# Last batch's down projection: each product of quarters made by seven products of sixteenths, weights stationary

## The chip, the core and the metric

The kernel runs on one core of a Trainium2 chip. TensorE (PE) multiplies matrices: it holds a stationary operand (`lhsT`), streams a moving one (`rhs`) past it, and adds up into PSUM. VectorE (DVE), ScalarE (ACT) and GpSimd (POOL) work element by element; POOL here works on SBUF only. SyncE (SP) issues most DMA transfers; ACT and POOL can issue some. Each engine works through its own queue in order and waits on semaphores of the others. The metric is the device time of one execution in microseconds.

## The reference

Attention with a mask by clusters, over 4 batches, 8 heads, 768 tokens and head size 64, and then a feed-forward block on the 3072 x 512 result:

```python
mask = q_assign[:, :, :, None] == k_assign[:, :, None, :]
scores = np.where(mask, scale * q @ k.T, -1e9)      # q, k: (4, 8, 768, 64)
x = softmax(scores) @ v                             # then bridged to (3072, 512)
h = x @ w_in                                        # w_in: (512, 2048)
g = h - np.tanh(h)
out = g @ w_out                                     # w_out: (2048, 512)
```

The change touches only the last line, and only for the last of the four batches (768 of the 3072 tokens). Everything is float32.

## The kernel before, in words

The feed-forward block is made batch by batch. Batch 0's second half and batches 1 to 3 use a Strassen-like scheme of seven products instead of eight: the matrices are cut into quarters, sums of quarters are made, seven products of quarters are computed, and the results are put together from them. The numbers 1 to 7 in `PRODUCTS` (L783) name the products.

For batches 1 to 3, `strassen_items(b)` (L992) lists the work as items. Its first 56 items are the up projection (`up_items`, L901): 8 blocks of rows `i`, seven products each, every product four matmul calls of 128x64 weights against 384 tokens (L933). The weights come as a *stream*: ready-made sums, one tile per block, fetched two ahead by `fetch_factors` (L844) on SP's queue into three buffers. VectorE evicts each product from PSUM and adds (L928). `shrink` (L997) makes tanh on ACT (L1000) and subtracts on POOL (L1002), and `done` (L1004) has POOL make one sum and one difference of quarters (L1007, L1008). The result lies in `G`, 2 x 2 quarters of 8 x 128 rows and 384 tokens, and in `S1` (`left1`).

Then come 21 items of the down projection: 7 products by 3 chunks of 128 tokens, `down_product` (L1014). There `G` or `S1` is stationary (128x64 halves) and the stream of w_out's sums is moving, 256 columns (L1029). Each item writes one PSUM tile (three buffers, `ps_f`). VectorE, or ACT for product 1 (L1035), evicts it into `du` or into `c` (L1040), POOL updates two quarters of `G` in place (L1036 after product 1, L1052 after product 2), and `put` sends finished 128 x 256 pieces to `out` (L1048), for the last batch by SP. All sums that this scheme needs of w_out are made once, early, and lie in DRAM (`down_factors`).

For batches 1 and 2 these items are threaded between the steps of the next batch's attention. For batch 3 nothing is left beside them: from L1376 on, the list `tail` runs alone, up projection first, then down projection, with a few checks between. The order of the instructions on each engine is the order in which the program emits them (a manual schedule). An item emits its matmuls, then its evictions; waits come from the data and from the buffers.

At the end of the program every engine waits for its queue, reads a flag and branches (L1561, L1562) past a general version.

Of the kernel before, what the change touches and what calls it, by code (L numbers as in the profile page):

```python
# [30 lines left out]
F32 = mybir.dt.float32  # L31
# [4 lines left out]
ALU = mybir.AluOpType  # L36
# [3 lines left out]
P = 128  # L40
# [18 lines left out]
def kernel(  # L59
# [10 lines left out]
    nc = tc.nc  # L70
# [3 lines left out]
    B, H, S, D = q.shape  # L74
# [3 lines left out]
    NCH = S // P  # L78
# [100 lines left out]
    def fast():  # L179
# [602 lines left out]
        HM = DM // 2  # L782
        PRODUCTS = (1, 2, 6, 7, 4, 5, 3)  # L783
        SLOT = {which: i for i, which in enumerate(PRODUCTS)}
        up_factors = dram.tile([HF, P, CH, 7, P], F32, name="up_factors", bufs=1)
        down_factors = dram.tile([7, P, HF, HM], F32, name="down_factors", bufs=1)

# [56 lines left out]
        def fetch_factors(n: int):  # L844

            if n < (B - 1) * PER:
                i = n + HF if n < 0 else n % PER
                t = streams[n] = late_pools["stream"].tile([P, HF, HM], F32, name="stream")
                if i < HF:
                    t = streams[n] = t.rearrange("p a b -> p (a b)")[:, 0 : 7 * CH * P].rearrange(  # L850
                        "p (c k f) -> p c k f", k=7, c=CH
                    )
                nc.sync.dma_start(t, up_factors[i] if i < HF else down_factors[i - HF])

        late_pools, half_pools, diffs = {}, {}, {}
        mid = ExitStack()
# [41 lines left out]
            ):  # L898
                nc.vector.tensor_tensor(out=out, in0=u, in1=w, op=ALU.subtract)  # L899

        def up_items(b: int, base: int, quarter, shrink, done):  # L901


            held = {}
            width = TB if b else TB // 2

            def up_product(i: int, k_: int, between):
                which = PRODUCTS[k_]
                x = [columns(b, c) for c in range(CD)]
                d = diffs[b] if which in (4, 5, 6) else None  # L910
                if which in (4, 5, 6):
                    right = [d[:, {5: 0, 6: 1, 4: 2}[which], c] for c in range(CH)]
                else:
                    rows_, half = {1: (0, 0), 2: (CH, 0), 3: (CH, 1), 7: (0, 1)}[which]
                    right = [x[rows_ + c][:, half] for c in range(CH)]
                if k_ == 0:
                    if b:
                        held[i] = (
                            late_pools["s"].tile([P, width], F32, name="s"),
                            late_pools["u"].tile([P, 2, width], F32, name="u"),  # L920
                        )
                    else:
                        t = turnp0.tile([P, 2, TB], F32, name="t1")
                        held[i] = t[:, 0, 0:width], t[:, 1].rearrange("p (a n) -> p a n", a=2)
                s, u = held[i]

                def add(out, x, y):
                    nc.vector.tensor_tensor(out=out, in0=x, in1=y, op=ALU.add)  # L928

                ps = ps_f.tile([P, TB], F32, name="pu", tag="f")[:, 0:width]  # L930
                for c in range(CH):
                    for r in halves:
                        nc.tensor.matmul(  # L933
                            ps[r], lhsT=streams[base + i][:, c, k_, r], rhs=right[c],
                            start=(c == 0), stop=(c == CH - 1),
                        )
                if which == 1:
                    nc.scalar.copy(out=s, in_=ps)
                elif which == 2:
                    add(quarter(i, 0, 0), ps, s)  # L940
                    if i == HF - 1:
                        shrink(i, 0, slice(0, 1))
                elif which == 6:
                    fetch_factors(base + i + 2)
                    add(u[:, 0], ps, s)
                elif which == 7:
                    add(u[:, 1], ps, u[:, 0])
                elif which == 4:
                    add(quarter(i, 1, 0), ps, u[:, 1])
                elif which == 5:  # L950
                    add(u[:, 0], ps, u[:, 0])
                    add(quarter(i, 1, 1), ps, u[:, 1])
                    shrink(i, 1, slice(0, 2))
                else:
                    add(quarter(i, 0, 1), ps, u[:, 0])

                    shrink(i, 0, slice(1 if i == HF - 1 else 0, 2))
                between()
                if k_ == len(PRODUCTS) - 1:
                    done(i)  # L960
                    streams.pop(base + i)


            return [
                (1.3 * width / TB, 1, lambda between, i=i, k_=k_: up_product(i, k_, between))
                for i in range(HF) for k_ in range(len(PRODUCTS))
            ]
# [6 lines left out]
        def half_up_items(gs):  # L974
# [13 lines left out]
                nc.gpsimd.tensor_tensor(out=t, in0=t, in1=th, op=ALU.subtract)  # L988

            return start_without(up_items(0, -HF, quarter, shrink, lambda i: None))  # L990

        def strassen_items(b: int):  # L992
            base = (b - 1) * PER
# [20 lines left out]
            def down_product(k_: int, j: int, between):  # L1014
# [49 lines left out]
                between()  # L1064


            return up_items(b, base, lambda i, f, t: G[:, i, f, t], shrink, done) + [
                (3.4, 2, lambda between, k_=k_, j=j: down_product(k_, j, between))
                for k_ in range(len(PRODUCTS)) for j in range(HCH)
# [526 lines left out]
```

## Time and profile before

| | |
|---|---|
| median of 3 runs | 957.5 us (956.85 to 958.44) |
| the profiled execution | 958.52 us, span of its instructions 956.7 us |
| PE busy | 941.8 us (98%) |
| DVE / ACT / POOL busy | 571.2 / 292.6 / 512.1 us |
| granted TensorE clock | 1.000 |
| last batch's up projection begins | at 805.38 us of the span |
| its down projection begins | at 877.98 us |
| the last eviction begins | at 950.71 us |

In the profile, "L1029 PE MATMUL pd<-stream,G 128*64 128x256 f32 x1728 | 191.2, 379" reads: line 1029 of the kernel, engine, operation, output tile and inputs, shapes, how many records, then busy time in us and the mean duration of one in ns. A float32 matmul call leaves two matmul records, each with a weight load of its own (PEld). "[2.31 <-ACT th L1000]" says that the engine stood idle for 2.31 us before, and what ended it. In a row of windows the columns are: stretch, its length, then busy us and number of instructions of PE, PEld, DVE, ACT and POOL, the granted clock, the share of DMA and GB/s.

### The profile page before, as it was taken

Reading aid. Unit: us, or ns where it says so; the run is one execution under the profiler, and the core shown is the slowest. Engines: PE = TensorE matmul, PEld = TensorE weight load, DVE = VectorE, ACT = ScalarE, POOL = GpSimd, SP = SyncE. Lnnn points to the kernel's source line nnn. Section 1 sums busy time; section 2 is a strip of 40 time slices with the busy share of each in tenths; the row PEclk is TensorE's granted clock in tenths of the full one; section 3 lists DMA queues with packets and bytes.
Section 4 is the critical chain, followed back from the end, with each engine's and each line's share of the span. In section 5 each row is a group of like instructions: output and inputs, shape, how many; then the busy total and the mean of one; then the engine's idle time right before and its main releaser. Section 6 shows DMA issues by size and latency. Waiting matters only on the chain.

```text
span 956.7 us, 16942 instructions
## 1 busy us (share of the span) xinstructions
PE 941.8 (98%) x6584; PEld 458.6 (48%) x6584; DVE 571.2 (60%) x1098; ACT 292.6 (31%) x453; POOL 512.1 (54%) x364
## 2 busy tenths in 40 slices
PE   8999999999999999999999999999999999999997
PEld 5433443345653333444455554444455555445664
DVE  7657676976776677666845567766754346443011
ACT  5575554223332332323321212333331220222000
POOL 1026353456775464777684453867796353657500
PEclk9999999999999999999999999999999999999999
DMA  7766455992736645474574746457334223323321
GB/s 196 200 188 147 141 153 128 261 258 88 196 117 157 158 143 122 151 175 130 189 191 148 181 146 184 111 179 173 110 125 146 98 81 103 116 78 132 107 106 36
DMA packets 166764, 139.85 MB, mean 146 GB/s; under 512 B 116580, under 2 KB 145044, under 8 KB 163988
## 3 DMA queue, kind: packets, MB, share of 16 engines
q1 hardware_dynamic: 160292, 117.15, 44.4%
q0 software_dynamic: 6240, 21.50, 6.8%
q8 instruction: 54, 0.88, 0.4%
q14 instruction: 34, 0.28, 0.1%
q10 hardware_dynamic: 144, 0.03, 0.0%
HBM read 117.48 MB, written 21.17 MB: 145 GB/s over the span
## 4 chain that ended last, share of the span: by engine, by line
PE 92%; DVE 2%; DMA 1%; ACT 1%; issue 1%; SPq 0%; DVEq 0%; ACTq 0%
PE pu L933 26%; PE pd L1029 23%; PE sc L499 14%; PE av L556 13%; PE o L746 8%; PE h L730 4%; PE sim L376 1%; DMA stream<-up_factors 1%; PE den L571 1%; PE den L617 1%; DVE e L531 1%; PE den L590 1%; DVE diff L899 0%; PE pq L432 0%; DVE t L348 0%
## 5 line engine op out<-in xcount | busy, mean ns | idle before, releaser
L547 POOL TENSOR_TENSOR sum<-sum,e 128x768 f32<-128x768 f32 x112 | 207.4, 1852 | 94.4 <-DVE e L531 90.2
L531 DVE SCALAR_TENSOR_TENSOR e<-row,code,sc 128x384 f32<-128x384 bf16 x336 | 185.9, 608 | 67.3 <-ACT sc L521 59.7
L521 ACT ACTIVATE sc<-sc 128x768 f32<-128x768 f32 x168 | 125.9, 789 | 229.5 <-PE sc L499 211.8
L1029 PE MATMUL pd<-stream,G 128*64 128x256 f32 x1728 | 191.2, 379 | 0.0
L933 PE MATMUL pu<-xT,stream 128*64 128x384 f32 (+1 forms) x1024 | 159.0, 447 | 1.7 <-DMA stream<-up_factors 1.1
L1029 PEld LDWEIGHTS pd<-stream,G 128*64 128x64 f32 x1728 | 123.9, 137 | 66.9 <-issue 7.2
L499 PE MATMUL sc<-t,t 64*128 64x384 f32 x768 | 150.2, 509 | 0.4 <-ACT e L521 0.3
L556 PE MATMUL av<-e,vals 128*64 128x384 f32 x768 | 145.9, 499 | 1.3 <-DVE e L531 1.3
L1002 POOL TENSOR_TENSOR G<-G,th 128x768 f32<-128x768 f32 (+1 forms) x51 | 87.1, 1724 | 69.4 <-ACT th L1000 69.2
L933 PE MATMUL pu<-diff,stream 128*64 128x384 f32 (+1 forms) x768 | 121.1, 448 | 2.8 <-DVE G L928 1.8
L933 PEld LDWEIGHTS pu<-xT,stream 128*64 128x64 f32 x1024 | 73.1, 137 | 75.8 <-issue 61.4
L499 PEld LDWEIGHTS sc<-t,t 64*128 64x128 f32 x768 | 65.9, 186 | 73.8 <-issue 37.6
L556 PEld LDWEIGHTS av<-e,vals 128*64 128x64 f32 x768 | 46.9, 136 | 86.3 <-issue 82.0
L1000 ACT ACTIVATE th<-G 128x768 f32<-128x768 f32 (+1 forms) x51 | 40.9, 806 | 148.9 <-DVE G L928 144.2
L543 POOL TENSOR_TENSOR sum<-e 128x768 f32<-128x768 f32 x28 | 52.6, 1879 | 62.8 <-DVE e L531 42.2
L746 PE MATMUL o<-w_out,g 128*64 128x512 f32 x384 | 86.1, 593 | 0.0
L933 PEld LDWEIGHTS pu<-diff,stream 128*64 128x64 f32 x768 | 53.8, 137 | 59.3 <-issue 45.2
L928 DVE TENSOR_TENSOR G<-pu,u 128x384 f32<-128x384 f32 x72 | 39.7, 552 | 32.9 <-PE pu L933 32.9
L1040 DVE SCALAR_TENSOR_TENSOR c<-pd,du 128x256 f32<-128x256 f32 x36 | 15.2, 421 | 67.1 <-PE pd L1029 67.1
L746 PEld LDWEIGHTS o<-w_out,g 128*64 128x64 f32 x384 | 27.4, 137 | 50.1 <-issue 50.0
L1040 DVE SCALAR_TENSOR_TENSOR du<-pd,du 128x256 f32<-128x256 f32 x27 | 11.4, 420 | 60.8 <-PE pd L1029 60.8
L730 PE MATMUL h<-xT,w_in 128*64 128x384 f32 x256 | 42.8, 486 | 0.0
(137 smaller groups left out, 827.0 us busy)
## 6 DMA issues: line engine op xcount, KB each, us to landing
stream<-up_factors SPq DMA_DIRECT2D x32, 896.0 KB
stream<-down_factors SPq DMA_DIRECT2D x21, 1024.0 KB
raw<-in_moe_w_in_dram POOLq DMA_DIRECT2D x16, 512.0 KB, 5.0
raw<-in_moe_w_out_dram POOLq DMA_DIRECT2D x16, 512.0 KB, 4.7
again<-in_moe_w_in_dram SPq DMA_DIRECT2D x32, 256.0 KB
again<-in_moe_w_out_dram SPq DMA_DIRECT2D x32, 256.0 KB
vals<-in_v_dram SPq DMA_DIRECT2D x32, 192.0 KB
row<-q_codes SPq DMA_DIRECT2D x29, 192.0 KB
```

The source lines that it names most:

```text
L499: nc.tensor.matmul(sc[i][:, h, 0:TB], lhsT=turned[n, 1][r].rearrange("p a n -> p (a n)")[:, j * P : (j + 1) * P], rhs=turned[n, 0][r, half ...
L521: nc.scalar.activation(out=out, in_=sc[i][:, :, 0:TB], func=ACT.Exp, scale=SCALE)
L531: nc.vector.scalar_tensor_tensor(out=e[:, h].rearrange("p (j n) -> p j n", n=P), in0=rows[n, half][:, h], scalar=(codes[n][:, h, 1, j : j ...
L543: nc.gpsimd.tensor_tensor(out=s, in0=pair[0], in1=pair[1], op=ALU.add)
L547: nc.gpsimd.tensor_tensor(out=s, in0=s, in1=pair[i], op=ALU.add)
L556: nc.tensor.matmul(avs[n, half][h * D : h * D + D], lhsT=vals[n][:, h, j], rhs=e[i][:, h], start=(j == 0), stop=(j == NCH - 1),)
L730: nc.tensor.matmul(h[r], lhsT=w_in[i][:, c, o * P : (o + 1) * P][:, r], rhs=xT[c][:, half], start=(c == 0), stop=(c == CD - 1),)
L746: nc.tensor.matmul(acc[sub][r], lhsT=gs[f % HF][:, f // HF, sub * P : (sub + 1) * P][:, r], rhs=w_out[f // FQ][:, f % FQ], start=(f == seq ...
L933: nc.tensor.matmul(ps[r], lhsT=streams[base + i][:, c, k_, r], rhs=right[c], start=(c == 0), stop=(c == CH - 1),)
L1000: nc.scalar.activation(out=th, in_=t, func=ACT.Tanh)
L1002: nc.gpsimd.tensor_tensor(out=t, in0=t, in1=th, op=ALU.subtract)
L1029: nc.tensor.matmul(ps[r], lhsT=left(i)[:, r], rhs=t[:, i], start=(i == 0), stop=(i == HF - 1))
```

## The change

Only the last batch's down projection is made in another way (`wide_items`). Each of the seven products of quarters is itself computed by seven products of sixteenths, in the same scheme one level deeper: 49 parts instead of 21 items. A part multiplies 192 tokens by 4 x 128 rows by 128 columns. The operands change sides: a sixteenth of the w_out stream is stationary (128x64 halves), and the tokens are moving, so a part comes out with output columns on partitions and tokens along them. PSUM tiles rotate over six buffers of three pools.

The sums of sixteenths are not in DRAM; they are made on the fly. For the next product, POOL makes four right-hand sums (`right_sums`, 512 elements per partition each) from its stream, and VectorE makes four left-hand sums (`left_sums`, 768 elements each), the third of them on POOL in two of the seven products. All of these have both inputs in SBUF. POOL's updates of `G` after products 1 and 2 are cut in four pieces of 768 elements each. The first product's sums are made during the up projection on VectorE (`aside`). For that the blocks are visited in the order 0, 4, 1, 5, 2, 6, 3, 7, and the products come in the order 1, 7, 2, 6, 4, 5, 3.

The seven parts of a product are added by VectorE on their way out of PSUM, ACT taking the first. The products are joined by VectorE sums of 768 elements (`joins`). As the result lies turned, VectorE turns it back in blocks of 32 x 32 (`transpose`), and it is stored in transfers whose pieces are 32 floats, four per half of a quarter on SP. The last quarter goes in four pieces, shared by SP and ACT.

Within a product, the work that is not needed at once (joins, left-hand sums) is spread over the seven parts behind their evictions. The diff, cut to its core:

```diff
+        BLOCKS = tuple(i + k_ * HF // 2 for i in range(HF // 2) for k_ in range(2))
+        WIDE = (1, 7, 2, 6, 4, 5, 3)
+        PARTS = (1, 2, 6, 7, 5, 4, 3)
...
-                nc.sync.dma_start(t, up_factors[i] if i < HF else down_factors[i - HF])
+                if i < HF:
+                    nc.sync.dma_start(t, up_factors[BLOCKS[i] if last else i])
+                else:
+                    nc.sync.dma_start(t, down_factors[SLOT[WIDE[i - HF]] if last else i - HF])
...
+            def left_sums(k_: int, engine, i=None):
...
+                l11, l12, l21, l22 = (left(k_, t, f, i) for t in range(2) for f in range(2))
+                return [
+                    lambda e=e, out=out, x=x, y=y, op=op: e.tensor_tensor(out=out, in0=x, in1=y, op=op)
+                    for e, out, x, y, op in (
+                        (nc.vector, s[5], l21, l22, ALU.add),
+                        (nc.vector, s[6], s[5], l11, ALU.subtract),
+                        (engine, s[7], l11, l21, ALU.subtract),
+                        (nc.vector, s[3], l12, s[6], ALU.subtract),
+                    )
+                ]
...
+            def right_sums(k_: int, engine):
...
+                r11, r12, r21, r22 = (right(k_, f, n) for f in range(2) for n in range(2))
+                return [
+                    lambda out=out, x=x, y=y: engine.tensor_tensor(
+                        out=out, in0=x, in1=y, op=ALU.subtract
+                    )
+                    for out, x, y in (
+                        (t[5], r12, r11), (t[6], r22, t[5]), (t[7], r22, r12), (t[4], r21, t[6]),
+                    )
+                ]
+
+            def aside(at: int, k_: int):
+                if at % 2 == 0 and at and 2 <= k_ < 6:
+                    left_sums(0, nc.vector, at // 2 - 1)[k_ - 2]()
+                if at == HF - 1:
+                    if k_ == 2:
+                        aux["right"] = right_sums(0, nc.vector)
...
+            def updates(which: int):
+                x, y = {1: ((0, 0), None), 2: ((1, 0), (0, 0))}[which]
+                def chunk(i: int):
+                    ks = slice(2 * i, 2 * i + 2)
+                    a = G[:, ks, x[0], x[1]]
+                    if y is None:
+                        nc.gpsimd.tensor_tensor(out=a, in0=left1[:, ks], in1=a, op=ALU.subtract)
...
+            def store(t: int, m: int, n: int, x=None):
...
+                for a in range(P // BL):
+                    queue = nc.scalar if x is not None and a % 2 else nc.sync
+                    queue.dma_start(out_b[b, t, m, n, a, :, ks], q_[a * BL : (a + 1) * BL, n, ks])
...
+            def part(k_: int, slot: int):
+                kind, final = PARTS[slot], k_ == len(WIDE) - 1
+                if slot == 0:
+                    fetch_factors(base + HF + k_ + 2)
+                    ready_ = joins(k_ - 1) if k_ else []
...
+                    if not final:
+                        for it in right_sums(k_ + 1, nc.gpsimd):
+                            it()
+                        ready_ += left_sums(k_ + 1, nc.vector if changed else nc.gpsimd)
+                    if k_ and WIDE[k_ - 1] in changed:
+                        for it in updates(WIDE[k_ - 1]):
+                            it()
...
+                for i in range(KH):
+                    for r in range(2):
+                        nc.tensor.matmul(
+                            ps[r * D : r * D + D], lhsT=w[:, i, r * D : r * D + D], rhs=x[:, i],
+                            start=(i == 0), stop=(i == KH - 1),
+                        )
...
+                def add(out, y):
+                    nc.vector.scalar_tensor_tensor(
+                        out=out, in0=ps, scalar=float(words), in1=y, op0=ALU.mult, op1=ALU.add
+                    )
...
+                ready_ = aux["ready"]
+                share = -(-len(ready_) // (len(PARTS) - slot))
+                for it in ready_[:share]:
+                    it()
+                del ready_[:share]
...
+            if b == B - 1:
+                aside, items = wide_items(b, base, G, left1)
+                return up_items(
+                    b, base, lambda i, f, t: G[:, i, f, t], shrink, done, BLOCKS, aside
+                ) + items
```

## The prediction

> **What bounds the kernel now.** I read four views. First the page: its slices say TensorE is busy everywhere at the full granted clock, so the end moves only with TensorE's work or with a new wait on it.
>
> ```profile
> PE   8999999999999999999999999999999999999997
> PEclk9999999999999999999999999999999999999999
> ```
>
> Second, the chain that ended last, from 860 us on: one up projection, then 72.5 us of down products without a gap, one eviction, the end. The waits ahead of the last batch cannot move by this edit.
>
> ```profile
> 859.76 18.38 PE pu L933 x114
> 878.14 72.54 PE pd L1029 x672
> 950.69 0.02 issue
> 950.71 0.42 DVE c L1040
> ```
>
> Third, the timeline of the stage. On TensorE the down projection starts at 877.98 (call it T0) and the last eviction starts at 950.71, so it takes 72.7 us. On POOL, work of the up projection reaches 5.9 us into it. The 7 us of updates behind that, three of L1036 and later three of L1052, end early.
>
> ```profile
> 878.94 2.77 POOL L1002 TENSOR_TENSOR G<-G,th 128x768 f32<-128x768 f32 x2 [2.31 <-ACT th L1000]
> 881.79 1.00 POOL L1007 TENSOR_TENSOR S<-G 128x384 f32<-128x384 f32 x1
> 882.87 1.00 POOL L1008 TENSOR_TENSOR G<-G 128x384 f32<-128x384 f32 x1
> 883.95 7.00 POOL L1036 TENSOR_TENSOR G<-S,G 128x1024 f32<-128x1024 f32 x3
> ```
>
> The windows show what room each engine has there: VectorE 9 us and POOL 19 us of 73.
>
> ```profile
> 878.00:951.00 73.00, 72.67 (x674) 48.11 (x670) 9.06 (x22) 2.50 (x5) 18.86 (x10) 1.00 0.27 93
> ```
>
> Fourth, because the edit fills that room with additions on both engines, I looked up what an addition costs on VectorE while POOL adds. L692 adds 128x384, SBUF with SBUF:
>
> ```profile
> L692 DVE TENSOR_TENSOR xT<-xT,den x19: 550/1402/2178, 62.1 to 794.4; 128x384 f32<-128x384 f32 x19
> ```
>
> The same addition takes 0.55 or 2.18 us. The timeline tells when:
>
> ```profile
> 182.42 1.81 POOL L547 TENSOR_TENSOR sum<-sum,e 128x768 f32<-128x768 f32 x1 [3.49 <-DVE e L531]
> 182.72 0.60 DVE L531 SCALAR_TENSOR_TENSOR e<-row,code,sc 128x384 f32<-128x384 bf16 x1
> 183.24 1.40 DVE L692 TENSOR_TENSOR xT<-xT,den 128x384 f32<-128x384 f32 x1
> ...
> 182.42 3.90 POOL L547 TENSOR_TENSOR sum<-sum,e 128x768 f32<-128x768 f32 x2 [3.49 <-DVE e L531]
> ```
>
> L531, with one input in PSUM, runs beside POOL at its usual 0.60. L692, with two inputs in SBUF, starts at 183.24, but ends at 184.64, 0.41 after POOL's addition (184.23): its 384 elements only run then. POOL's second addition, which is next, ends at 186.32, 1.68 after L692. So additions with two SBUF inputs and POOL's additions take turns, whole instruction by whole instruction.
>
> **The change part by part.** Each product of quarters (384 tokens x 1024 x 256; 3 x 32 matmul records) becomes seven parts (192 tokens x 512 x 128) of 16 records.
>
> *TensorE, if nothing waits.* The shape "weights 128x64 stationary, 192 tokens moving" exists in the first batch:
>
> ```profile
> 235.35 0.82 PE L933 MATMUL pu<-xT,stream 128*64 128x192 f32 x8
> 236.00 1.47 PE L933 MATMUL pu<-diff,stream 128*64 128x192 f32 x16
> 237.30 0.82 PE L933 MATMUL pu<-xT,stream 128*64 128x192 f32 x8
> ```
>
> Sixteen records take 1.30 us from start to start, so 49 parts take 63.7 us, 9.0 less than the 72.7. The Trainium skill, "TensorE: Matmul & The Clock Gate", Part 3, The mechanism, has a rule against this: a weight load overlaps running matmuls only where its row group differs, and these use all rows. By it 784 loads of about 53 ns (the same page's columns / 1.2, an estimate) would lie bare, some 42 us, and the sum would end near 1000. Here the row decides: weight loads of 137 ns stand beside records 81 ns apart, so they overlap, and I add nothing.
>
> *Additions.* All take turns unless an input is in PSUM. POOL's cost by size: 0.59 us for 192 elements, 1.00 for 384, 1.82 for 768, 2.37 for 1024 (rows L988, L1007, L1002, L1036), a line that gives 1.27 for 512. VectorE: 0.355 for 192 and 0.55 for 384 (L899), the data alone 0.40 by the turn shown; so about 0.95 for 768, and 0.82 directly behind a POOL turn.
> After T0, up to the last left-hand sum, POOL has the leftovers 1.82 + 3 x 1.00 = 4.8; right-hand sums of six products, 6 x 4 x 1.27 = 30.5; two left-hand sums, 3.6; the updates of G after products 1 and 2, now eight of 768, 14.5. That is 53.4 in 38 instructions, with gaps of 0.07 (as between its rows) 56.1. VectorE has 22 left-hand sums of 768 and five joins, 27 x 0.82 = 22.1, and the last four small left-hand sums of the first product, 0.9: 23.0. POOL starts 1.0 after T0. At about 29 of VectorE's turns POOL's set-up and gap fall under the turn: 1.82 - 1.68 + 0.07 = 0.21 each, 6.1. Sum: 1.0 + 56.1 + 23.0 - 6.1 = 74.0.
> TensorE alone would ask for that last sum, the third left-hand sum of product 3 and last in POOL's queue, at 45 x 1.30 = 58.5. It comes 15.5 late, four parts (itself, 5, 4, 3) follow, 5.2, and TensorE ends at T0 + 79.2: 6.5 us later than now instead of 9.0 earlier.
> That these turns follow each other closely I checked against the order of the queues. POOL never runs dry: the right-hand sums of product k+1 are queued at the start of product k, and their stream was fetched a product earlier. VectorE stands in line behind POOL's current instruction, and the evictions queue behind it. Six PSUM buffers let TensorE run on for 6 x 1.30 = 7.8 us, so an eviction is rarely what TensorE waits for. It waits for sums, first at the third and fourth part (6, 7) of a product, and at the start of product 6 for the update.
>
> *The end.* Now, TensorE's end to SP's last issue is 0.8 us, then 5.2 to the end of the span. The turned output is stored as 40 transfers of 128-byte pieces instead of 12 of 1 KB; eight go by ACT. Once the last left-hand sum is made, VectorE has two joins, nine evictions, eight transposes (0.95 per 768 by L348, so 0.35 at most) and some small adds waiting, and reaches the two halves of quarter (1,1) about 2 and 0.4 us before TensorE ends, at T0 + 77.3 and 78.9. From there SP has 14 issues in a row. L1048 issues in 0.33 (128 pieces); x<-in_q (L340, 768 pieces of 128 bytes) takes 0.31 at least, 0.79 in the median, 0.42 at the head of a burst. I take 0.41 plus a gap of 0.04, the head's, as these have half the pieces or fewer: 77.3 + 6.3 = 83.6, against 73.5 now. Ends: 14 x 0.37 gives 82.5, 14 x 0.83 gives 88.9. The landing, at most 1.4 us behind the issue, still lies under the 2.9 us for which SP's branch waits at the end.
>
> *At nothing:* the new order of blocks and of streams (same 896 and 1024 KB, same queue); the small sums in the up projection, which take turns with POOL too (VectorE is busy 27.5 us of 63 there; an eviction may come 1.8 us late, and TensorE has three buffers, two parts of 1.29 us, in hand; what waits of the first product's parts 2 and 6 lies inside the turns summed above); ACT's seven short copies. Stores now stand ahead of two fetches on SP; a stream has a whole product, 10 us, to land.
>
> *Sum:* 83.6 - 73.5 = 10.1 us. The profiled execution took 958.5 (span 956.7) and would take 968.6; the median of the runs shown is 957.5, so 967.6.
>
> **The rivals.**
> 1. *The turns do not bind* (the other side). If 768-element sums run beside POOL, each sum is ready a part before use: 63.7 + 0.2 and an end of 1.3 to 4 give SP 65.9 to 68.5, 5 to 7.6 less: 951. It decides if VectorE's L1047 rows (after's left sums) stand near 0.95 instead of 1.5 to 2.6. Against it: every L692, L831 and L899 that meets a POOL addition in the trace is stretched, or stretches it (L711, 1.36 instead of 1.00).
> 2. *The stores set the end.* With 0.79 per issue the last 14 take 11.6: 15.4 more, 973. For it: the L340 median. Against: those come in bursts of eight with twice to four times the pieces.
> 3. *Fewer turns:* if the turns sum to 64 instead of 74.0, as when POOL's rows with strided halves cost a seventh less than the line through its rows, the time is 957.5, no change. Against it: the strided updates of now (L1036, 2.37) lie on that line.
>
> One price stands only on a page: "TensorE: Matmul & The Clock Gate", What's actually happening, halves TensorE's clock after about 3.4 us idle. I expect one wait near 4 us, so by it the sum would be up to 1.7 more; the granted clock is 1.00 all through this trace, and no gap here is long enough to show it.
>
> **How the numbers follow.** Forecast 0.73 (its own range 962 to 971: 5% on POOL's rows is 3 us either way, SP's issues -1 to +3); rival 2 0.13; rival 1 0.11; rival 3 0.03. Within 0.2% (1.9 us, what a measurement of this kernel can tell): 0.03; faster 0.11; slower 0.86. The range leaves out rivals 1 and 3 and the outer edges: 960 to 975.
>
> **What would show it.** Right: TensorE's busy share in the last 80 us well under 0.9, waits of parts 6 and 7 on DVE and POOL sums, each product 10 to 12 us long, POOL busy almost without a gap to T0 + 74, left-hand sums 1.5 to 2.6 us, and a rush of store issues after TensorE's end. Wrong: parts 1.30 us apart to the end, or left-hand sums of 0.95 beside POOL.

## The result and the profile after

The changed kernel takes 971.6 us (971.28 to 971.98, 4 runs), the kernel before 957.9 beside it (956.85 to 958.44, 4 runs): a ratio of 1.0145, 95% interval 1.0127 to 1.0162. It is 14 us slower. The forecast was 967.6, so slower, with a range of 960 to 975. The profiled execution took 971.82, with a span of 970.0.

The page of the changed kernel has the loss in its last four slices of 24 us: TensorE is no longer busy everywhere, and POOL is busy throughout three of them.

```profile
PE   8999999999999999999999999999999999998983
DVE  6657677976767587566645487666844356549794
POOL 1025343556664556775984454777784453669991
PEclk9999999999999999999999999999999999999997
```

The timeline of TensorE in the stage gives the two ends. A row is start, duration, engine, line, operation, records, and in brackets the idle time before it.

```profile
877.04 2.77 PE L1190 MATMUL pw<-G,stream 128*64 128x192 f32 x32
879.64 1.47 PE L1190 MATMUL pw<-e,again 128*64 128x192 f32 x16
...
888.93 1.47 PE L1190 MATMUL pw<-e,xT 128*64 128x192 f32 x16
892.88 2.34 PE L1190 MATMUL pw<-t,xT 128*64 128x192 f32 x16 [2.48 <-POOL t L1047]
894.99 2.38 PE L1190 MATMUL pw<-e,xT 128*64 128x192 f32 x16
897.21 1.47 PE L1190 MATMUL pw<-G,du 128*64 128x192 f32 x16
...
936.65 1.76 PE L1190 MATMUL pw<-e,xT 128*64 128x192 f32 x16 [2.18 <-DVE e L1047]
938.60 2.78 PE L1190 MATMUL pw<-t,xT 128*64 128x192 f32 x16 [0.19 <-DVE t L1047]
941.19 1.50 PE L1190 MATMUL pw<-e,xT 128*64 128x192 f32 x16
...
953.16 1.47 PE L1190 MATMUL pw<-t,stream 128*64 128x192 f32 x16
```

The stage starts at 877.04 (T0 of this kernel) and its last part at 953.16. With the 1.30 us of a part, TensorE ends at 954.46, 77.4 after T0. Before, it was 950.69 - 877.98 = 72.7. Parts that wait for nothing start 1.30 apart (877.04 plus two parts is 879.64). So the arithmetic alone is faster, as forecast: 49 parts at 1.30 are 63.7. The stage takes 13.7 more. Of these 8.1 are waits, listed here, and the rest is lost in the parts around them, most of it behind the two longest waits: parts of 2.11 and 2.22 us from 892.88 on, and of 1.76 and 2.59 from 936.65 on.

```profile
PE pw L1190 <- POOL t L1047: 2.5, 1, 2.5
PE pw L1190 <- DVE e L1047: 2.4, 2, 2.2
PE pw L1190 <- DVE c L1198: 2.0, 3, 0.9
PE pw L1190 <- DVE t L1047: 1.2, 2, 1.0
```

Three of the four are left-hand sums (L1047), the third is evictions. The timeline of VectorE and POOL shows why the sums are late:

```profile
888.35 2.00 POOL L1074 TENSOR_TENSOR du<-stream,xT 128x512 f32<-128x512 f32 x1
...
890.19 0.97 DVE L1047 TENSOR_TENSOR e<-G 128x768 f32<-128x768 f32 x1
890.31 2.51 POOL L1047 TENSOR_TENSOR t<-G 128x768 f32<-128x768 f32 x1
891.09 0.35 DVE L1198 SCALAR_TENSOR_TENSOR sum<-pw,c 128x192 f32<-128x192 f32 x1
891.35 2.28 DVE L1047 TENSOR_TENSOR e<-e,G 128x768 f32<-128x768 f32 x1
892.78 1.98 POOL L1074 TENSOR_TENSOR again<-stream 128x512 f32<-128x512 f32 x1
```

VectorE's sum of 768 takes 0.97 where it starts as one POOL addition ends (890.19), and 2.28 where it starts during the next (891.35): POOL's addition ends at 892.82, VectorE's at 893.63, 0.81 later. POOL's next one is stretched to 1.98. The eviction between them, which reads PSUM, takes its usual 0.35. The window of the stage, in the columns of the profile before (after the length: PE, PEld, DVE, ACT, POOL), has VectorE at 66 us instead of 9 and POOL at 70.5 instead of 19:

```profile
878.00:952.00 74.00, 65.88 (x746) 56.18 (x742) 66.15 (x86) 2.73 (x8) 70.51 (x38) 0.95 0.28 83
952.00:970.00 18.00, 2.63 (x34) 2.01 (x29) 5.51 (x18) 0.00 (x0) 0.00 (x0) 0.67 0.30 48
```

The second part of the loss lies behind TensorE's end. Of SP's queue, the last stores before the change, then the timeline of the changed kernel from 953.8 and the waits at its end (total us, times, longest):

```profile
923.54 27.96 SPq L1048 DMA_DIRECT2D out_dram<-c  x9
```

```profile
953.82 10.87 SPq L1128 DMA_DIRECT2D out_dram<-vals  x14
```

```profile
SPq L1128 <- DMA out_dram<-vals: 3.4, 3, 2.2
```

Fourteen stores are issued one after the other from 953.82 to 964.69, which is 10.2 us behind TensorE's end; before, SP's last issue ended 0.8 us behind it (951.50). Of the three waits, the two long ones are for stores that ScalarE issued: the two queues share eight semaphores on which landings are counted (a semaphore is a counter that an engine can wait for). SP's issues at 957.84 and 960.36 wait for the semaphores of ScalarE's stores of 956.34 and 956.70, which the trace has landing at 957.82 and 960.34.

The account of the two spans: the stage starts 0.94 earlier; TensorE takes 77.4 instead of 72.7, +4.7; its end to SP's last issue takes 10.2 instead of 0.8, +9.4; from there to the end of the span 5.3 instead of 5.2, +0.1. The sum is +13.3, which is 970.0 - 956.7. Two thirds of the loss lie behind TensorE's end, one third is TensorE's.

### The profile page after: what moved, and what is told of

Same layout as the page of the kernel before. It is cut to its first block, busy times and chain, and to the rows that moved or that the text cites. A ratio compares the mean times of both kernels' runs of the same rounds, so it can differ in the third digit from the quotient of the medians.

```text
span 970.0 us, 17381 instructions
## 1 busy us (share of the span) xinstructions
PE 937.5 (97%) x6696; PEld 469.4 (48%) x6696; DVE 641.0 (66%) x1195; ACT 294.0 (30%) x457; POOL 566.2 (58%) x392
## 4 chain that ended last, share of the span: by engine, by line
PE 82%; DVE 6%; POOL 3%; issue 3%; DMA 1%; ACT 1%; SPq 0%; DVEq 0%; POOLq 0%; ACTq 0%
PE pu L944 25%; PE pd L1280 15%; PE sc L499 13%; PE av L556 13%; PE o L746 6%; PE h L730 4%; PE sim L376 1%; DVE e L531 1%; POOL G L1103 1%; PE den L571 1%; PE den L617 1%; DMA stream<-up_factors 1%; DMA up_factors<-made 1%; DVE t L1047 1%; DVE x L1112 1%
## 5 line engine op out<-in xcount | busy, mean ns | idle before, releaser
L1280 PE MATMUL pd<-stream,G 128*64 128x256 f32 x1152 | 128.7, 379 | 0.0
L1280 PEld LDWEIGHTS pd<-stream,G 128*64 128x64 f32 x1152 | 82.5, 137 | 45.9 <-issue 6.8
L939 DVE TENSOR_TENSOR u<-pu,u 128x384 f32<-128x384 f32 x48 | 26.5, 552 | 15.8 <-PE pu L944 15.6
L1299 POOL DMA_DIRECT2D out_dram<-c x24 | 13.4, 557 | 39.7 <-DVE c L1291 39.6
```

The costliest lines, as they stand in the source:

```text
L1280: nc.tensor.matmul(ps[r], lhsT=left(i)[:, r], rhs=t[:, i], start=(i == 0), stop=(i == HF - 1))
```

## The experiments

The theory (A) is that of the prediction: VectorE's additions of two SBUF inputs and POOL's additions take turns, so the sums come late; then the small stores lengthen the end. The rivals were that the mere number of sums on the two engines sets the pace, that the lower clock behind TensorE's wait is the loss, that the stores are hidden, and that their cost is not in the issuing. In what follows T0 is the start of the first part of each run, TensorE's end is the start of the last part plus 1.30, and the tail runs from there to the end of SP's last store issue. Where ScalarE's last store comes later, it is by 0.3 us at most, except where the text or the table says so. The kernel before stood at 956.9 to 957.8 beside these runs, and the changed kernel was not run beside them again, so a difference of 1 us between two rows is read from the ratios.

| run | TensorE's end after T0 | tail | time (us) | ratio to before, 95% |
|---|---|---|---|---|
| before | 72.7 | 0.8 | 957.9 | |
| changed kernel | 77.4 | 10.2 | 971.6 | 1.0127 to 1.0162 |
| e1_long_stores | 77.4 | 3.7 (ScalarE's last: 5.0) | 965.2 | 1.0068 to 1.0102 |
| e3_psum_input | 64.4 | 7.9 | 957.0 | 0.9987 to 1.0006 |
| e7_psum_and_long | 64.3 | 3.0 | 952.0 | 0.9918 to 0.9950 |
| e5_two_queues | 77.4 | 7.0 | 968.3 | 1.0098 to 1.0132 |
| e4_right_on_dve | 78.5 | 8.5 | 971.0 | 1.0129 to 1.0163 |
| g1_right_dve_two_queues | 77.6 | 6.3 | 967.1 | 1.0095 to 1.0128 |
| f1_psum_left | 87.0 | 6.3 | 976.8 | 1.0190 to 1.0225 |
| f2_two_queues | 88.7 | 2.3 | 975.0 | 1.0158 to 1.0196 |
| f5_four_whole | 64.8 | 8.6 | 957.2 | 0.9985 to 1.0004 |
| f3_psum_five | 65.8 | 6.8 | 954.6 | 0.9958 to 0.9983 |
| f3_again | 65.7 | 6.6 | 956.4 | 0.9976 to 0.9999 |
| f4_three_queues | 65.7 | 4.0 (ScalarE's last: 6.9) | 955.1 | 0.9961 to 0.9983 |

### The turns alone: e3_psum_input

```diff
+ z = aux["still"].unsqueeze(1).to_broadcast([P, KH, TH])   # a PSUM tile, set to 0 once
...
- lambda e=e, out=out, x=x, y=y: e.tensor_tensor(out=out, in0=x, in1=y, ...)   # left-hand sums
+ lambda e=e, out=out, x=x, y=y: e.tensor_tensor(
+     out=out, in0=z if e is nc.vector else y, in1=x, op=ALU.add)
...
- turn_ = (k_ * len(PARTS) + slot) % 6
+ turn_ = (k_ * len(PARTS) + slot) % 5
```

> Edit: in products 2 to 7 of the last batch each left-hand sum on VectorE reads a constant tile of zeros in PSUM in place of one of its two inputs in SBUF; count, size and queue of all additions stay, and POOL's are untouched. One PSUM buffer of six is given up for it. Left out: one summand of each of these sums, so the output is not the reference's. Theory A (an addition of two SBUF inputs on VectorE and an addition on POOL take turns): VectorE's left-hand sums of 768 fall from 1.5 to 2.3 us to 0.95, POOL's sums of 512 all stand at 1.27 instead of 1.27 to 2.00, POOL's queue ends near T0 + 58 instead of T0 + 72, and TensorE ends at T0 + 64 to 67 instead of T0 + 77.4. The tail of stores stays, so the time is 959 to 962. Rival B (it is the count of sums on the two engines, in what order they stand, not turns): rows of both engines as in the changed kernel, TensorE's end at T0 + 76 to 79, time 970 to 973. Rival C (the lower granted clock behind TensorE's wait of 2.5 us is the main loss): only if that wait is gone does the time fall, and then by 2 to 3 us, to 969.

Measured: 957.0 us (956.02 to 959.5), 2 us under the range of theory A, as the tail fell too, from 10.2 to 7.9. The timeline of VectorE and POOL at the place shown for the changed kernel:

```profile
888.37 1.83 POOL L1052 TENSOR_TENSOR t<-G 128x768 f32<-128x768 f32 x1
...
889.37 0.95 DVE L1052 TENSOR_TENSOR e<-still,e 128x768 f32<-128x768 f32 x1
890.14 1.29 POOL L1088 TENSOR_TENSOR again<-stream 128x512 f32<-128x512 f32 x1
...
890.60 0.95 DVE L1052 TENSOR_TENSOR t<-still,G 128x768 f32<-128x768 f32 x1
```

VectorE's sums take 0.95 in the middle of POOL's additions, and POOL's additions, whose code is the same, take 1.83 and 1.29 instead of 2.51 and 1.98. POOL's last sum and TensorE's last part, from their timelines, and TensorE's one wait in the stage:

```profile
933.31 1.84 POOL L1052 TENSOR_TENSOR t<-G 128x768 f32<-128x768 f32 x1
```

```profile
940.16 1.47 PE L1202 MATMUL pw<-t,stream 128*64 128x192 f32 x16
```

```profile
PE pw L1202 <- POOL xT L1088: 0.2, 1, 0.2
```

With T0 at 877.11, POOL is done at T0 + 58.0 instead of 72.1, and TensorE ends at T0 + 64.4 instead of 77.4. Counts, sizes and queues of the sums are those of the changed kernel; what differs is where one input lies, that zeros stand for a summand, so that a sum waits for one input less, and that there are five PSUM buffers instead of six. Mere counts do not set the pace, then. That the missing summand does not either is shown by f5_four_whole below, which has the whole computation and ends at T0 + 64.8. It also measures TensorE's own work without waits: 64.4, where the prediction said 63.7. The Trainium skill, "GPSIMD Engine Reference", 1. Specifications, says that POOL shares its SBUF interfaces with VectorE and that this collides with VectorE instructions of two SBUF inputs. These rows agree and give the price that the page does not: 13 us in this stage.

### The stores alone: e1_long_stores

```diff
- for a in range(P // BL):
-     queue = nc.scalar if x is not None and a % 2 else nc.sync
-     queue.dma_start(out_b[b, t, m, n, a, :, ks], q_[a * BL : (a + 1) * BL, n, ks])
+ if x is None:                       # 128 partitions, pieces of 128 floats
+     nc.sync.dma_start(rows_.rearrange("(p k) c -> p k c", p=P), q_.rearrange("p (k c) -> p k c", c=P))
+     return
+ for i, queue in enumerate((nc.sync, nc.scalar)):
+     queue.dma_start(...)            # two halves of 64 partitions
```

> Edit: VectorE turns the last batch's output as in the changed kernel, but the turned tiles are stored as whole transfers in pieces of 512 bytes, 14 in place of 40. Left out: the pieces land at other places of the output, so the output is not the reference's; the bytes are the same. Theory A (turns of VectorE's and POOL's additions delay TensorE; after that the many small stores delay the end): TensorE still ends 77 us after the start of the stage (T0), VectorE's last turn still ends 80.6 after it (957.62 in the trace of the changed kernel), and SP's last issue comes about 1 us behind that instead of 7.1 behind: about 6 us less, 965.5. Rival S (stores are hidden behind something else, such as the landing): 971.6, no change. Rival W (it is the waits for earlier stores to land, 3.4 + 3 + 2.2 us in the trace, and not the issues): with 14 transfers on the same number of semaphores no transfer waits for an earlier one; the total is the same as in A, but single issues stay at 0.4 to 1.0.

Measured: 965.2 us (964.57 to 967.08), against 965.5 by theory A. SP's issues at the end, from its timeline:

```profile
953.37 2.26 SPq L1127 DMA_DIRECT2D out_dram<-vals  x2
955.88 1.87 SPq L1132 DMA_DIRECT2D out_dram<-vals  x3
```

SP's last issue ends at 957.75, 0.6 behind VectorE's last transpose (957.16), and ScalarE's at 959.09; TensorE's end stays at T0 + 77.4. So 6.4 us belong to the number and form of the stores, and the 3.7 that remain of SP's tail are mostly VectorE's evictions and transposes behind TensorE. None of SP's issues waits for an earlier transfer any more. (The expectation reads "3.4, 3, 2.2" in the row of SP's waits in the changed kernel as three waits; it is 3.4 us in three waits, the longest 2.2.) Waits and number of issues went together here, so this run does not part them.

### Both: e7_psum_and_long

The edit is the two above in one kernel.

> Edit: e3_psum_input and e1_long_stores together. Left out, as there: one summand of VectorE's left-hand sums of products 2 to 7 is zero, and the pieces of the last output land at other places. If turns and stores are the two causes and each acts on its own, their gains add: 971.6 less 14.6 (e3_psum_input) less 6.4 (e1_long_stores) is 950.6; TensorE ends at T0 + 64.4 and SP's last issue comes some 2 us after it. If the stores only cover other work that then shows (the landing, the joins on VectorE), the time stays above 953.

Measured: 952.0 us (950.56 to 952.34), 1.4 above the plain sum of the gains. The reason is in the table: the tail had already come down from 10.2 to 7.9 in e3_psum_input, so only 4.9 of it were left for the long stores to take. Without the two causes (and with the summands and places of the output that these edits leave out) the changed form of the product is 0.66% faster than before (0.50 to 0.82%). Rival 1 of the prediction put the case without turns at 951; it takes the long stores as well to come near that.

### The issuing queue: e5_two_queues

```diff
- queue = nc.scalar if x is not None and a % 2 else nc.sync
+ queue = nc.scalar if (x is not None or (t, m) == (1, 1)) and a % 2 else nc.sync
```

> Edit: the changed kernel, only the eight stores of the last quarter (1,1) alternate between SP's queue and ScalarE's instead of all going by SP's. Count, bytes and piece size stay. The tail from TensorE's end to SP's last issue was 10.2 us in the changed kernel, 3.7 with long stores. Theory I (the issuing engine sets the tail: 14 issues in a row on SP with waits between): SP's last issue comes 3 to 5 us earlier, time 966.5 to 968.5. Rival R (the 16 DMA engines' rate for 128-byte pieces sets it): the same as the changed kernel within 1 us, 970.6 to 972.6.

Measured: 968.3 us (966.56 to 968.76). SP's and ScalarE's stores of the end, from their timelines (SP's from 953.0, ScalarE's from 950.0):

```profile
953.57 7.60 SPq L1128 DMA_DIRECT2D out_dram<-vals  x10
```

```profile
951.92 9.54 ACTq L1128 DMA_DIRECT2D out_dram<-vals  x12
```

The same 24 transfers and bytes on the same DMA engines end 3 us earlier behind TensorE (7.0 on SP and 7.3 on ScalarE instead of 10.2), and SP's waits for earlier transfers fall from 3.4 to 1.7 us. So the rate of the DMA engines alone did not set the tail of the changed kernel; how the issues are spread over the queues did. The landing of stores has a part in it all the same: the waits that are left to SP here are for its own stores of 953.57 to 957.21, which land 2.0 to 3.3 us after their issue ended. The Trainium skill, "DMA: Bandwidth & Descriptors", Issuing engines are not separate DMA queues, says that a second issuing engine saves only the time to initiate the transfers, which is usually small beside the transfers. Here, with 128-byte pieces at the end of the kernel, it saved 3.3 us of 971.6 (2.9 by the ratios).

### Fewer additions on POOL: e4_right_on_dve and g1_right_dve_two_queues

```diff
- for it in right_sums(k_ + 1, nc.gpsimd):
-     it()
+ ready_ += right_sums(k_ + 1, nc.vector)
```

> Edit, with the whole computation kept: the 24 right-hand sums of 512 of products 2 to 7 move from POOL's queue to VectorE's, put among its other sums. Theory A (turns): the sum of the turns falls from 74 by about 24 x 1.30 (POOL's) and grows by about 24 x 0.55 to 0.7 (VectorE's), to some 56 to 60 us, under the 58.5 at which TensorE alone asks for the last sum, so TensorE ends at T0 + 64 to 68 instead of T0 + 77.4 and, with the same tail of stores, the time is 959 to 963. Rival V (VectorE's own queue becomes the bound: evictions stand behind sums that wait for a stream or a turn): TensorE waits for evictions and right-hand sums on VectorE, its end stays at T0 + 75 or later, time 969 or more.

> Edit: e4_right_on_dve with the alternating stores of e5_two_queues. If both causes are separate, their gains add: e4_right_on_dve's time less 3 to 5 us; by theory A and I, 955 to 959. If the stores' rate sets the end once TensorE is early, no gain over e4_right_on_dve.

Measured: 971.0 (970.84 to 971.69) and 967.1 us (966.94 to 968.95). For the first, theory A was used wrongly, and rival V holds. The window from T0 to the place where POOL ended in the changed kernel, and TensorE's main wait, in e4_right_on_dve:

```profile
878.00:949.00 71.00, 60.70 (x704) 56.09 (x702) 69.66 (x104) 3.51 (x9) 27.69 (x14) 0.95 0.28 86
```

```profile
PE pw L1189 <- DVE e L1047: 10.0, 5, 5.5
```

POOL falls to 27.7 us, but VectorE is busy for 69.7 of 71: it has 104 instructions where it had 82. The turns are mostly gone: 19 of VectorE's 22 left-hand sums of 768 take 0.94 to 0.95. Still TensorE ends at T0 + 78.5. The sum of turns that I worked out left out VectorE's evictions and transposes, which take no turn with POOL but do stand in VectorE's queue. Beside 24 more sums they make VectorE the bound. In the second run the alternating stores take off 3.8 us, against 3.3 alone: that gain adds.

### A version with the whole computation: f1, f2, f5, f3 and f4

ScalarE copies the quarters into PSUM, so that VectorE's left-hand sums have one input there.

```diff
+ def copied(x):
+     t = ps_s.tile([P, 2, 512], F32, name="held", tag="s")[:, :, 0:TB]
+     t = t.rearrange("p a (b n) -> p a b n", b=2)
+     nc.scalar.copy(out=t, in_=four(x))
+     return t
...
+ lambda: tensor(s[5], 21, l22, ALU.add),         # 21, 11, 12: the copies
+ lambda: tensor(s[7], l11, 21, ALU.subtract),
+ last_two,                                       # s[6] = s[5] - 11, and the copy 12
+ lambda: tensor(s[3], 12, s[6], ALU.subtract),
...
+ if (k_ * len(PARTS) + slot) % 2 == 0:
+     aux["pw"] = ps_f.tile([P, TB], F32, name="pw", tag="f")
+     ps = aux["pw"][:, 0:TH]
+ else:
+     ps = aux["pw"][:, TH:TB]
```

> Edit, with the whole computation kept: ScalarE copies three of the four quarters of each left-hand side (of products 2 to 7 of the last batch) into PSUM, VectorE makes all four left-hand sums of a product from one input in PSUM and one in SBUF, and none is left to POOL. The parts' results use two halves of each of three PSUM buffers. Theory A: VectorE's sums take about 0.95 each beside POOL, POOL keeps 24 sums of 512 at 1.27 and the updates, about 50 us in all, and TensorE ends at T0 + 64 to 67; with the tail of stores as in the changed kernel the time is 959 to 962. Rival B (counts, not turns): VectorE has two more sums and ScalarE 18 copies more, so the time is 971 or more. Rival D (the PSUM copies come late, as they stand in ScalarE's queue behind its other work): waits of TensorE on sums that wait for ScalarE, TensorE's end at T0 + 70 or later, time above 964.

> Edit: as f1_psum_left, and the eight stores of the last quarter (1,1) alternate between SP's queue and ScalarE's. Theory A: SP's issues at the end fall from 14 in a row to about 9, the tail of 10.2 us behind TensorE's end falls by 2.5 to 4, so 955 to 959, 3 to 4 below f1_psum_left. Rival W (the rate of small pieces at the 16 DMA engines sets the tail, not the issuing engine): the same as f1_psum_left within 1 us.

Measured: 976.8 (976.65 to 978.52) and 975.0 us (972.57 to 975.76), slower than the changed kernel. Both expectations of theory A were missed by 14 us or more. It is the time of rival B, but not its reason. From the waits of f1_psum_left and its groups by line (the column behind the second bar is the idle time before them):

```profile
PE pw L1222 <- DVE c L1230: 8.0, 10, 2.4
PE pw L1222 <- ACT c L1237: 4.0, 4, 1.9
PE pw L1222 <- DVE sum L1230: 3.9, 7, 0.6
PE pw L1222 <- DVE x L1230: 1.7, 2, 1.2
```

```profile
L1063 DVE TENSOR_TENSOR t<-held,e 128x768 f32<-128x768 f32 x6 | 5.7, 948 | 0.0
L1108 POOL TENSOR_TENSOR xT<-stream 128x512 f32<-128x512 f32 x6 | 7.6, 1270 | 0.0
```

The sums are as theory A has them, 0.95 on VectorE and 1.27 on POOL. What TensorE waits for is evictions: 17.6 us in 23 waits. A suspect was that a part writes the second half of a buffer whose first half is still to be read. The next run changes that alone.

```diff
- if (k_ * len(PARTS) + slot) % 2 == 0:
-     aux["pw"] = ps_f.tile([P, TB], F32, name="pw", tag="f")
-     ps = aux["pw"][:, 0:TH]
+ if (k_ * len(PARTS) + slot) % 4 < 3:
+     ps = ps_f.tile([P, TB], F32, name="pw", tag="f")[:, 0:TH]
  else:
-     ps = aux["pw"][:, TH:TB]
+     ps = ps_a.tile([P, TB], F32, name="pw", tag="a")[:, 0:TH]
```

> Edit, with the whole computation kept: f1_psum_left, only that a part's result lies in one of four whole PSUM buffers instead of one of six halves of three. Theory S (in f1_psum_left TensorE waited 18 us because a part may not write into the second half of a buffer while VectorE or ScalarE still has the first half to read): the waits for evictions mostly go, TensorE ends at T0 + 64 to 68 instead of T0 + 87.0, and with all the last stores on SP the time is 957 to 961. Rival H (the three copies on ScalarE and the sums that wait for them delay the evictions): TensorE still waits for evictions 10 us or more and ends at T0 + 75 or later, 967 or more.

Measured: 957.2 us (955.65 to 957.97), and of TensorE's waits in the stage one is left:

```profile
PE pw L1221 <- DVE x L1229: 0.8, 1, 0.8
```

So it was the sharing: four whole buffers are better than six halves, by 22.2 us of TensorE's end (T0 + 64.8 instead of 87.0). With only the sums and the buffers of the parts changed the kernel stands level with the kernel before: what TensorE gains, the tail of 8.6 us takes. f3_psum_five adds the alternating stores (and holds one copy at a time, in five whole buffers).

> Edit, with the whole computation kept: as f1_psum_left (ScalarE copies three quarters of the left-hand side of products 2 to 7 into PSUM one after the other, VectorE adds from there), but with one copy held at a time, the parts' results in five whole PSUM buffers instead of halves of three, and the stores of e5_two_queues. In f1_psum_left VectorE's sums of 768 took 0.95 and POOL's of 512 took 1.27 to 1.28, as theory A says, but TensorE waited 18 us for evictions of VectorE and ScalarE, where a part's result shared a buffer with the part before. Theory A with that cause: without shared buffers TensorE ends at T0 + 64 to 66, as in e3_psum_input (T0 + 64.4), and the stores on two queues take 3 to 5 us off its 957.0: 952 to 954, below the kernel before. Rival D (the copies on ScalarE in the way): waits on sums behind ScalarE, 958 or more.

> The kernel of f3_psum_five once more, unchanged, with more rounds: 954 to 955, ratio to the kernel before 0.996 to 0.998, TensorE's end at T0 + 65 to 66. If its lead was chance, the interval takes in 1.

> Edit, with the whole computation kept: f3_psum_five, with the last 16 stores (those of quarter (1,1) and of the last product) dealt in turn to SP's, ScalarE's and POOL's queues. POOL has no work left by then. Theory I (issuing and the waits for earlier stores of the same queue set the tail): five or six stores a queue instead of eight, the last issue 1 to 2 us earlier, 952.5 to 953.5. Rival G (POOL issues and completes transfers more slowly than SP and ScalarE, of which no row of the profile before tells): the same as f3_psum_five or up to 2 us slower.

The edit of f4_three_queues:

```diff
- queue = nc.scalar if (x is not None or (t, m) == (1, 1)) and a % 2 else nc.sync
+ queue = (
+     (nc.sync, nc.scalar, nc.gpsimd)[(4 * n + a) % 3] if x is not None or (t, m) == (1, 1) else nc.sync
+ )
```

Measured: f3_psum_five 954.6 us (952.76 to 955.66) and once more 956.4 (953.77 to 959.81), ratios 0.9970 and 0.9987, both intervals below 1 though the second time only just; f4_three_queues 955.1 (954.62 to 955.86), ratio 0.9972. These are the kernels with the whole computation that beat the kernel before, by 1 to 3 us. The first run was expected at 952 to 954 and the second at 954 to 955: both came out slower, so the lead is smaller than it looked. A third queue brought nothing that can be told from f3_psum_five, where 952.5 to 953.5 was expected of it. SP's and ScalarE's stores of the end, from the timeline of f4_three_queues:

```profile
940.05 6.57 SPq L1162 DMA_DIRECT2D out_dram<-vals  x9
940.06 9.43 ACTq L1162 DMA_DIRECT2D out_dram<-vals  x9
```

SP is done 2.2 us earlier than in f3_psum_five (946.62 against 948.82), but ScalarE's last two issues come no earlier (949.49). The trace tells why: the first of the two, at 948.67, waits for the semaphore of ScalarE's own store of 943.84, which lands only at 948.60, 4.3 us after its issue ended. The stores at the end of the changed kernel land 1.1 to 3.2 us after theirs. POOL's stores land no later than the others (1.3 to 4.2), so rival G's reason is not what is seen. From 948.60 to 951.12 the last twelve stores to land come some 0.2 us apart, whichever queue issued them. With three queues, then, ScalarE's last issues are held up by the landing; what sets the pace of the landing was not tested.

## Why the prediction was right, point by point

*TensorE's own work.* Right. The prediction had 63.7 for 49 parts at 1.30; e3_psum_input, with 0.2 us of waits, took 64.4. By the rule that a weight load overlaps only another row group, weighed there from the Trainium skill, "TensorE: Matmul & The Clock Gate", Part 3, The mechanism, the time would have been near 1000; the parts 1.30 apart show the loads hidden.

*The turns.* Right in mechanism, a little too large. The last left-hand sum on POOL was put at T0 + 74.0, and it ended at 946.62 + 2.53 = 949.15, T0 + 72.1. The 5.2 from there to TensorE's end are 5.3. So TensorE's end is at T0 + 77.4 instead of 79.2. In e3_psum_input, where VectorE's left-hand sums take no turn, POOL's last sum ends at T0 + 58.0. The prediction's terms for POOL alone, 1.0 + 56.1, give 57.1. So POOL was priced well, and the turns of the left-hand sums are worth 14.1, where the prediction had 16.9 (23.0 - 6.1) for these and the joins. Which of them were too dear was not measured one by one; the 22 rows go from 0.97 to 2.29, the first from a sum that met POOL between two instructions. The waits of TensorE were forecast at parts 6 and 7 for such sums; all five waits for sums in the list above are at these parts, and none is at the start of product 6, where one was forecast for the update. The products take 9.1 to 14.6 us, where 10 to 12 were forecast: the delay falls on some of them and not on all alike. Forecast as rare were the waits for evictions: 2.0 us in three.

*The end.* This is the step that was mis-sized: "14 issues in a row", at "0.41 plus a gap of 0.04", 6.3 us. The first of them came at T0 + 76.8, forecast as 77.3, but the fourteen took 10.87, or 0.78 each. The issues last 6.8 us in all (0.485 each, two of them 1.0 and the rest at 0.32 to 0.47), the gaps 0.7, and 3.4 are waits of SP for earlier stores to land, ScalarE's for the most part. The prediction had no such wait: it spoke of landing only behind the last issue, and put it at 1.4 us at most, where the stores at the end take 1.1 to 3.2. Rival 2, "The stores set the end", had 0.79 per issue. Its price was the true one, though its reason (long issues, from the median of another burst) was only a part of it. So the measured 971.6 lies nearer to rival 2's 973 than to the forecast's 967.6. e5_two_queues confirms that spreading the issues shortens this time.

*The sum.* The forecast had TensorE at 79.2 and SP at 83.6 after T0. Measured are 77.4 and 87.65, so errors of -1.8 and +5.8 (in what comes behind TensorE), and T0 itself was 0.94 earlier: 3.1 us in all. That is the 971.8 of the profiled execution against the forecast 968.6 for it. The median lies inside the range of 960 to 975, and 0.6 above the forecast's own 962 to 971. That it lies so near is partly luck: the store term was 5.8 too small, and errors of the other sign took back 2.7 of it.

*The rivals.* Rival 1's terms, 63.7 + 0.2 + 1.3 to 4, add up to 65.2 to 67.9, not to its 65.9 to 68.5, which changes little. The rival, that turns do not bind, was to be told by VectorE's L1047 rows at 0.95 instead of 1.5 to 2.6; most are 1.5 to 2.3. e3 and e7 show what that rival would have given: 957 with the stores, 952 without. The 1.3 to 4 us that it put for the end is what e7 has (3.0), not what the changed kernel's stores make (7.9 with an early TensorE). Rival 3, turns of 64 instead of 74.0, did not occur: they end at T0 + 72.1.

*What was costed at nothing.* The order of blocks, the sums in the up projection and ScalarE's copies show no wait of TensorE: none is in the list above, and from 800 us to the stage the list of TensorE's waits is empty for both kernels. That the stage starts 0.94 earlier than before is of the size by which T0 differs among the runs of this study (876.30 to 877.88).

## What to carry to other kernels

Before giving POOL and VectorE elementwise work side by side, find a pair of rows in the trace where they overlap, and add the two engines' times where both of VectorE's inputs lie in SBUF; moving one input to PSUM by an idle engine undid that here. Count the transfers at the end of a kernel as a queue with waits for the landing of earlier ones in it, also of those that another queue issued on the same semaphores: 0.78 us per store here, not the 0.45 of an issue and its gap. When a buffer is split to get more of them, check who waits for the whole.

## What was not expected of the hardware

*The clock behind a wait.* In the changed kernel, the two parts behind the 2.48 us wait at 892.88 take 2.11 and 2.22 instead of 1.30 (rows above). e1_long_stores has the same wait at the same place, from its timeline:

```profile
892.44 1.52 PE L1197 MATMUL pw<-t,xT 128*64 128x192 f32 x16 [2.47 <-POOL t L1047]
893.79 1.47 PE L1197 MATMUL pw<-e,xT 128*64 128x192 f32 x16
895.09 1.47 PE L1197 MATMUL pw<-G,du 128*64 128x192 f32 x16
```

There the parts keep to 1.30 to 1.35, and the granted clock from 890 to 900 us is 1.00, against 0.83 in the changed kernel. A second such stretch follows the 2.18 us wait before 936.65 (clock 0.89 from 930 to 940 us); e1_long_stores has that wait too, 2.18 us before 936.23, and its clock stays at 1.00. TensorE ends 77.4 after T0 in both: it was waiting for the sums anyhow (10.8 us in e1_long_stores, 8.1 in the changed kernel), so the lower clock cost nothing. The pair f1_psum_left and f2_two_queues differs in the same way at a wait of 2.42 and 2.43 us (clock 1.00 and 0.86 from 878 to 890 us). There TensorE waited for evictions of its own results, 18.0 us in sum in both runs, and the end was 1.7 us later, which is what a clock of 0.86 takes from 12 us. The Trainium skill, "TensorE: Matmul & The Clock Gate", What's actually happening, has the clock halved after an idle window of some 3.4 us that runs freely. That a wait of one length may or may not lower the clock fits a free-running window; that 2.2 to 2.5 us can be enough is what these rows add. The prediction expected one wait near 4 us and, by this page, up to 1.7 us for it; the longest wait is 2.48.

*Small stores.* At the end of the kernel, transfers of 128-byte pieces are issued in 0.315 to 0.485 us, at times in 1.0 to 1.9 (the longest in f1_psum_left), and land 1.1 to 3.2 us later in the changed kernel and up to 4.3 in f4_three_queues. SP's issue at 960.36 waited 2.2 us for a store of ScalarE's, as both queues count landings on the same semaphores.
